# Block-sparse attention with a feed forward: gathered keys per 32 queries, unnormalised probabilities, layer norm in token layout

## The chip, the cores and the metric

The kernel runs on one core of a Trainium2 chip. The metric is the device time of one execution in microseconds. The times of before are those of three runs; the profile is of one execution.

## The reference

Four batches, eight heads, 768 positions of 64 values; blocks of 32 positions (24 a sequence). A query sees its own block and its two neighbours, the first and the last block, and three sampled blocks per query block (the same for all heads); queries of the first and the last block see everything. Then the heads are joined to 512 channels, and a layer norm and a feed forward with a residual follow.

```python
scores = scale * np.matmul(q, k.transpose(0, 1, 3, 2))
mask = np.abs(blk_i - blk_j) <= window          # window 1
mask = mask | (blk_i == 0) | (blk_j == 0) | (blk_i == n_blocks - 1) | (blk_j == n_blocks - 1)
for qb in range(n_blocks):
    for kb in sampled_blocks[qb]:
        mask[qb * block:(qb + 1) * block, kb * block:(kb + 1) * block] = True
scores = np.where(mask, scores, -1000000000.0)
...
attn = attn / (np.sum(attn, axis=-1, keepdims=True) + 1e-09)
...
xn = (x - mu) / np.sqrt(var + 1e-06) * g_ln
ch = np.maximum(xn @ w_ch1, 0.0) @ w_ch2        # 512 -> 2048 -> 512
return (x + ch).astype(np.float32)
```

## The kernel before

All matrix products are of fp16 halves: a float32 value is split in a high and a low half, and three of the four products are summed (high by high, high by low, low by high).

A **slot** is one head and 128 queries; there are 192, in order of batch, of three chunks of 256 queries (a **unit**, twelve in all), of pairs of heads. In a slot all 768 keys are scored: line 274 multiplies the stacked halves of q by the high and low halves of k, line 280 adds the low half of q by the high half of k. The result `ps` has 128 x 768. `softmax_a` adds the mask as a bias per key block (`allow`) and finds the guard of the exponent with one custom VectorE instruction (line 289), ScalarE takes the exponential with its row sum (293). `softmax_b` makes the reciprocal and a normalised high half `ph` (306), `softmax_c` the low half `pl` (314, in some slots on GpSimd, 312), and two DMA transpositions issued from SP (320, 321) put both, keys on partitions, in `pt`. `attn_v` multiplies the values by them a pair of heads at a time (332, 337), the two heads in two 64-wide column tiles, into `pa` with channels on partitions.

`layer_norm` works with channels on partitions: sums over channels are matmuls with ones (367 to 370). `ffn` is a generator that gives one matmul a step: the first layer (424) into `pu`, halves of the hidden values (434, 435), the second layer (466, 450) into `pd` with channels on partitions, the sum with the residual (409) and the store (411).

The order of issue: the main loop walks over slots. In each it issues the scores of this slot, the softmax steps of the slot before, and then a mixture of steps of the attention queue and of the feed-forward queue; `NFF` is 16 steps a slot. TensorE stands in the order as written, SP and GpSimd too in the first 27 slots; the rest is ordered by the scheduler. The loads of q, k, v, w1 and w2 are generators in an agenda by slot; k and q are cast by the GpSimd DMA queue and the low halves subtracted. Both weight matrices come as float64 bits and are split in the first 36 slots.

## Time and profile before

| | |
|---|---|
| median of 3 runs | 906.25 us (905.23 to 913.89) |
| the profiled execution | 913.7 us span, 913.89 us its own time |
| TensorE busy | 804.4 us, 6576 matmuls |
| VectorE, ScalarE, GpSimd busy | 691.0, 529.9, 288.4 us |
| DMA | 131.34 MB in 341896 packets |

Busy times are unions, so matmuls that overlap count once. Group rows give the line, the engine, the operation, the tiles, the count, the busy time, the mean of one in ns, and the idle time just before with what ended it. A matmul's mean duration contains its latency; the rate is read from start to start in the timeline. Timeline rows give the start and the length in us.

### The profile page before, as it was taken

The page shows a single profiled execution, that of the slowest core. Times are in us where ns is not written, and L with a number is a line of the kernel's source. Part 1 is how long each engine was busy: PE and PEld are TensorE (multiplying, and loading weights), DVE is VectorE, ACT ScalarE, POOL GpSimd, SP SyncE. Part 2 cuts the span into 40 slices and gives each one's busy share as a digit, 9 for nine tenths or more (in the row PEclk, how much of TensorE's full clock was granted, in tenths as well). Part 3 has the DMA queues.
Part 4 walks back from the last instruction along what each step waited for, and adds up shares of the span by engine and source line. Part 5 has one row for each costly group of instructions (what it writes and reads, how often), then busy time and mean ns, then how long its engine had stood idle before and what let it go on. Part 6 is the DMA issues. An engine that isn't in the chain of part 4 may idle for free.

```text
span 913.7 us, 17727 instructions
## 1 busy us (share of the span) xinstructions
PE 804.4 (88%) x6576; PEld 554.9 (61%) x6576; DVE 691.0 (76%) x1400; ACT 529.9 (58%) x914; POOL 288.4 (32%) x301
## 2 busy tenths in 40 slices
PE   3345568887888999999899999999999999999998
PEld 0011235554655677766567767776677777777887
DVE  6979899996467888788588788788888887883320
ACT  3566766766456765656585666656766665662120
POOL 5483656585532111154431101336321100000000
PEclk9976669997999999999989999999999999999999
DMA  8899797999997887899977776999898776662000
GB/s 214 205 261 216 148 235 188 203 177 131 165 165 141 142 126 131 135 172 178 162 126 143 141 126 127 153 163 167 161 130 145 122 118 119 105 113 42 19 6 25
DMA packets 341896, 131.34 MB, mean 144 GB/s; under 512 B 311600, under 2 KB 331184, under 8 KB 341808
## 3 DMA queue, kind: packets, MB, share of 16 engines
q1 hardware_dynamic: 329280, 108.06, 63.3%
q0 software_dynamic: 11712, 22.03, 14.2%
q8 instruction: 52, 0.85, 0.4%
q14 instruction: 36, 0.29, 0.1%
q10 hardware_dynamic: 816, 0.11, 0.1%
HBM read 60.92 MB, written 6.29 MB: 74 GB/s over the span
## 4 chain that ended last, share of the span: by engine, by line
PE 50%; DVE 7%; DMA 7%; ACT 3%; issue 3%; SPq 0%; ACTq 0%; DVEq 0%
PE pd L466 20%; PE pu L424 18%; PE pa L332 4%; DMA pt<-pl 4%; PE ps L274 3%; DMA pt<-ph 3%; PE ps L280 2%; DVE pl L314 2%; PE pa L337 2%; DVE p L289 2%; ACT p L293 2%; ACT ph L306 1%; DVE hl L435 1%; DVE xc L394 1%; DVE mua L353 0%
## 5 line engine op out<-in xcount | busy, mean ns | idle before, releaser
L314 DVE SCALAR_TENSOR_TENSOR pl<-p,st,ph 128x768 f16<-128x768 f32 x177 | 211.9, 1204 | 77.8 <-ACT ph L306 41.0
L293 ACT ACTIVATE p<-p,st 128x768 f32<-128x768 f32 x192 | 178.6, 930 | 113.9 <-DVE st L289 108.9
L306 ACT ACTIVATE ph<-p,st 128x768 f16<-128x768 f32 x177 | 162.4, 927 | 60.2 <-DMA pt<-ph 44.5
L466 PE MATMUL pd<-hl,w2h 128*128 128x256 f16 x704 | 192.4, 273 | 1.4 <-DVE hl L435 1.4
L466 PE MATMUL pd<-hh,w2h 128*128 128x256 f16 x704 | 192.7, 274 | 0.0
L466 PE MATMUL pd<-hh,w2l 128*128 128x256 f16 x704 | 192.4, 273 | 0.0
L289 DVE CUSTOM_DVE_ANT_1 p<-ps,allow 128x768 f32<-128x768 f32 x192 | 177.4, 951 | 10.4 <-PE ps L280 9.4
L424 PEld LDWEIGHTS <-w1h 128*128 128x128 f16 x1536 | 146.3, 99 | 59.5 <-issue 41.8
L274 PE MATMUL ps<-kx,qx 128*128 128x512 f16 (+1 forms) x384 | 92.3, 350 | 75.1 <-DVE st L289 57.8
L466 PEld LDWEIGHTS <-w2h 128*128 128x128 f16 x1408 | 133.6, 98 | 37.2 <-issue 22.7
L424 PE MATMUL pu<-xh,w1h 128*128 128x256 f16 x768 | 118.9, 278 | 12.8 <-DVE hl L435 8.8
L424 PE MATMUL pu<-xl,w1h 128*128 128x256 f16 x768 | 123.8, 278 | 3.0 <-DVE xl L398 3.0
L424 PE MATMUL pu<-xh,w1l 128*128 128x256 f16 x768 | 123.4, 279 | 0.0
L263 POOL TENSOR_TENSOR ql<-qr,qx 64x256 f16<-64x256 f32 x94 | 76.1, 809 | 112.3 <-issue 39.5
L332 PE MATMUL pa<-pt,vh 128*64 128x512 f16 x576 | 110.4, 408 | 0.7 <-DMA pt<-pl 0.7
L216 POOL DMA_DIRECT2D qx<-qT x48 | 26.8, 560 | 242.7 <-PE ps L274 137.1
L434 ACT ACTIVATE hh<-pu 128x512 f16<-128x512 f32 x96 | 56.2, 585 | 77.1 <-PE pu L424 77.1
L274 PEld LDWEIGHTS <-qx 128*128 128x128 f16 x384 | 37.1, 100 | 102.2 <-issue 76.9
L435 DVE SCALAR_TENSOR_TENSOR hl<-pu,hh 128x512 f16<-128x512 f32 x96 | 65.7, 685 | 30.9 <-ACT hh L434 30.6
L424 PEld LDWEIGHTS <-w1l 128*128 128x128 f16 x768 | 75.2, 100 | 18.9 <-issue 9.2
L337 PE MATMUL pa<-pt,vl 128*64 128x256 f16 x576 | 84.2, 287 | 0.0
L466 PEld LDWEIGHTS <-w2l 128*128 128x128 f16 x704 | 68.9, 98 | 15.4 <-issue 7.7
(95 smaller groups left out, 933.6 us busy)
## 6 DMA issues: line engine op xcount, KB each, us to landing
qr<-qs SPq DMA_DIRECT2D x48, 128.0 KB, 3.1
kx<-kT POOLq DMA_DIRECT2D x16, 384.0 KB, 6.3
qx<-qT POOLq DMA_DIRECT2D x48, 128.0 KB, 3.5
raw<-w SPq DMA_DIRECT2D x12, 512.0 KB, 4.3
out<-ot SPq DMA_DIRECT2D x48, 128.0 KB, 2.4
vr<-v POOLq DMA_DIRECT2D x24, 192.0 KB, 3.7
raw<-ks POOLq DMA_DIRECT2D x12, 384.0 KB, 4.4
w2l<-w SPq DMA_DIRECT2D x4, 1024.0 KB, 6.2
```

What stands on the lines that cost most here:

```text
L263: eng.tensor_sub(ql[rows], qr[rows], qx[rows, j])
L274: nc.tensor.matmul(s.ps[:, lo:hi], qx[:, s.h % 2, s.qs], kx[:, s.h % 2, lo:hi], start=True, stop=False)
L289: nc.vector.tensor_tensor_reduce(out=s.p.rearrange(blk, k=BLK), in0=s.ps[:, 0:S].rearrange(blk, k=BLK), in1=bias, scale=-0.125, scalar=3.0 ...
L293: nc.scalar.activation(s.p, s.p, AF.Exp, bias=s.st[:, 0:1], scale=-1.0, accum_out=s.st[:, 2:3])
L306: nc.scalar.activation(ph, s.p, AF.Copy, scale=st[:, 3:4])
L314: nc.vector.scalar_tensor_tensor(out=pl, in0=s.p, scalar=st[:, 3:4], in1=ph, op0=ALU.mult, op1=ALU.subtract)
L332: nc.tensor.matmul(pa[hh * D : (hh + 1) * D, 0 : 2 * CH], vh[:, hh, t, :], pts[hh][:, t].rearrange("p i n -> p (i n)"), start=t == 0, stop ...
L337: nc.tensor.matmul(pa[hh * D : (hh + 1) * D, 0:CH], vl[:, hh, t, :], pts[hh][:, t, 0, :], start=False, stop=t == KT - 1, skip_group_check= ...
L424: nc.tensor.matmul(ph[:, j * CH : (j + 1) * CH], w[:, ct, fs], x[:, ct, :], start=n == 0, stop=n == 3 * CT - 1, skip_group_check=True)
L434: nc.scalar.activation(dh, ph[:, 0 : 2 * CH], AF.Relu)
L435: nc.vector.scalar_tensor_tensor(out=dl, in0=ph[:, 0 : 2 * CH], scalar=0.0, in1=dh, op0=ALU.max, op1=ALU.subtract)
L466: nc.tensor.matmul(po, w[:, f, es], x[:, f, :], start=n == 0, stop=n == 3 * FT - 1)
```

## The change

The kernel is rewritten around **units of 32 queries**. 88 units (blocks 1 to 22 of four batches) make 22 sparse tiles of four units; the queries of the first and last blocks make two dense tiles. A **slot** is one tile and head: 24 x 8 = 192 and a pause of 8.

- Scores: a unit's keys are its 256 own ones. Three neighbouring blocks are read where the keys lie (`kx`), the first, the last and the three sampled blocks are copied beside each other (`kg`) by `gather_k`, one tile ahead: 16 copies from SP, 12 of them from an address that SP first reads as a register (`value_load`). Each unit is a matmul of 32 columns wide output (tile of 32 partitions in PSUM).
- Values are split, written to DRAM with both halves in a row (`vrow`), and the 256 rows of a unit are fetched by two indirect DMAs of GpSimd (`gather_v`, 8 a tile).
- Softmax: the exponent carries the factor 4096, the halves `ph` and `pl` are those of the unnormalised exponential, made for a pair of heads at once, and the reciprocal is applied after the product with the values, which now has tokens on partitions.
- Layer norm by VectorE's statistics instructions with tokens on partitions; its halves are transposed by DMA for the first layer. g is folded into w1. The second layer has the hidden values as the stationary operand and 512 output channels as columns: 1152 matmuls of 512 columns instead of 2304 of 256.
- SP, GpSimd and TensorE stand in the written order throughout the main loop. All keys of a batch are loaded before its first slot. Feed forward begins in slot 27, 24 steps a slot, 384 steps for a group of two tiles (16 slots); a second-layer matmul counts two steps.

```diff
+    LAG = 6
+    FF0 = 27
+    NFF = 24
...
+    def gather_k(t):
...
+        t.kg = kgp.tile([P, 4, 5, H * BLK], F16, tag="kg", name=f"kg{t.i}")
+        for u, (b, i) in enumerate(t.units):
+            kx = kx_s[b % 2]
+            nc.sync.dma_start(t.kg[:, u, 0:2, :], kx[:, 0 : NB : NB - 1, :])
+            for r in range(NR):
+                n = (i - 1) * NR + r
+                reg = nc.sync.value_load(ss_i[0:1, n : n + 1, 0], min_val=0, max_val=NB - 1)
+                nc.sync.dma_start(t.kg[:, u, 2 + r : 3 + r, :], kx[:, bass.ds(reg, 1), :])
...
+    def gather_v(t):
+        t.vg = vgp.tile([P, 4, 2, H, P], F16, tag="vg", name=f"vg{t.i}")
+        for u, (b, i) in enumerate(t.units):
+            for j, idx in enumerate((ia, ib)):
+                nc.gpsimd.indirect_dma_start(
+                    t.vg[:, u, j].rearrange("p h d -> p (h d)"), None, vrow[b],
+                    bass.IndirectOffsetOnAxis(ap=idx[:, i - 1 : i].bitcast(U32), axis=0),
+                )
...
+        for n, q in enumerate((t.qx, t.ql)):
+            for k in range(2):
+                for u, (b, i) in enumerate(t.units):
+                    rows = slice(u * BLK, (u + 1) * BLK)
+                    if k == 0:
+                        dst, rhs = pr.ps[rows, h % 2, 0:3], kx_s[b % 2][:, i - 1 : i + 2, hs]
+                    else:
+                        dst, rhs = pr.ps[rows, h % 2, 3:8], t.kg[:, u, :, hs]
+                    nc.tensor.matmul(dst, q[:, h, rows], rhs,
+                                     start=n == 0 and k == 0 and h % 2 == 0,
+                                     stop=n == 1, skip_group_check=True)
...
+        for k in range(n):
+            nc.scalar.activation(pr.e[:, k], pr.e[:, k], AF.Exp, bias=st[:, 1, h0 + k : h0 + k + 1],
+                                 scale=-1.0, accum_out=st[:, 2, h0 + k : h0 + k + 1])
...
+        nc.scalar.copy(pr.ph, e)
+        nc.vector.tensor_sub(pr.pl, e, pr.ph)
...
+    def transposes(pr):
+        n, W = len(pr.heads), S if pr.t.kind == "d" else 256
+        pr.pT = ptp.tile([P, 2, n * W // P, P], F16, tag="pt", name=f"pt{pr.i}")
+        nc.sync.dma_start_transpose(out=pr.pT[:, 0], in_=pr.ph)
+        nc.sync.dma_start_transpose(out=pr.pT[:, 1], in_=pr.pl)
...
+        for k in range(nk):
+            for i in range(2):
+                for rows, vv in parts:
+                    w = D if i else P
+                    nc.tensor.matmul(t.xa[rows, h % 4, 0:w], pr.pT[:, i, k0 + k, rows],
+                                     vv[:, k, 0:w], start=first and k == 0 and i == 0,
+                                     stop=k == nk - 1 and i == 1, skip_group_check=True)
...
+        nc.vector.bn_stats(ls[:, 0:6], x)
+        nc.vector.bn_aggr(ls[:, 8:10], ls[:, 0:6])
...
+    def ln_transposes(gr):
+        gr.xT = lnp.tile([P, 2, CT, 2 * P], F16, tag="xT", name=f"xT{gr.i}")
+        for j, t in enumerate(gr.tiles):
+            ts = slice(j * P, (j + 1) * P)
+            nc.sync.dma_start_transpose(out=gr.xT[:, 0, :, ts], in_=t.xh)
+            nc.sync.dma_start_transpose(out=gr.xT[:, 1, :, ts], in_=t.xl)
...
+                for n, (w, x) in enumerate(((w2h, hh), (w2l, hh), (w2h, hl))):
+                    nc.tensor.matmul(po, x[:, f, ts], w[:, f, :], start=f == 0 and n == 0,
+                                     stop=f == FT - 1 and n == 2)
+                    if f < FT - 1 or n < 2:
...
+    for t in tiles:
+        if t.i:
+            at(once(gather_k, t), t.first - (4 if t.n == 5 else 7))
+        if t.i > 1:
+            at(once(load_q, t), t.first - 6)
...
+            at(once(gather_v, t), t.first - 2)
...
+            run(i)
+            if i < NS and slots[i]:
+                scores(slots[i])
+                pr = slots[i].pr
+                if slots[i] is pr.slots[-1]:
+                    softmax(pr)
+            if 0 < i <= NS and slots[i - 1] and slots[i - 1] is slots[i - 1].pr.slots[-1]:
+                transposes(slots[i - 1].pr)
+            if 0 <= i - LAG < NS and slots[i - LAG]:
+                s = slots[i - LAG]
+                attn_v(s)
+                if s.h == H - 1:
+                    gr = groups[s.t.i // 2]
+                    layer_norm(s.t, gr, s.t.i % 2)
+                    if s.t.i % 2:
+                        lnq.append((i + 1, gr))
```

What stands on SP in the middle of the program before: the transpositions of the probabilities (`pt`), now and then a store (`out`) or a load of q (`qr`).

```order
L320 DMA_TRANSPOSE pt_4_4435<-ph_4431 128x6x128
L411 DMA out<-ot_0_4402 128x256
L321 DMA_TRANSPOSE pt_4_4435<-pl_4433 128x6x128
L320 DMA_TRANSPOSE pt_5_4498<-ph_4494 128x6x128
L321 DMA_TRANSPOSE pt_5_4498<-pl_4496 128x6x128
L411 DMA out<-ot_1_4531 128x256
L256 DMA qr_5631<-qs 128x256
```

And on SP in the middle of the changed program, at the end of a group of two tiles: a store, the probabilities of the third pair of heads, the four transpositions of the layer norm (`xT`), those of the fourth pair, and the beginning of the next tile's run of key copies (`kg`).

```order
L471 DMA out<-x_4987 128x512
L374 DMA_TRANSPOSE pt_6957<-ph_6883 128x4x128
L375 DMA_TRANSPOSE pt_6957<-pl_6884 128x4x128
L427 DMA_TRANSPOSE xT_6978<-xh_6321 128x4x128
L428 DMA_TRANSPOSE xT_6978<-xl_6322 128x4x128
L427 DMA_TRANSPOSE xT_6978<-xh_6913 128x4x128
L428 DMA_TRANSPOSE xT_6978<-xl_6914 128x4x128
L374 DMA_TRANSPOSE pt_7100<-ph_7034 128x4x128
L375 DMA_TRANSPOSE pt_7100<-pl_7035 128x4x128
L274 DMA kg_7146<-kx_130 128x2x256
L277 TENSOR_LOAD ss_i
L277 ISA x2
```

The run then goes on with twelve such register loads (`ss_i` holds the numbers of the sampled blocks) and sixteen copies up to the next load of q; before, nothing but single loads and stores stood between two transpositions.

TensorE of the changed program at the same place, where the probabilities by values of a tile's first head (`pa`) end and the first layer of a new group (`pu`) begins:

```order
L395 MATMUL pa_0_6961<-vg_6352,pt_6723 32x64
L395 LDWEIGHTS pt_6723
L395 MATMUL pa_0_6961<-vg_6352,pt_6723 32x64
L444 LDWEIGHTS w1h
L444 MATMUL pu_0_6985<-xT_6978,w1h 128x256
```

Both read a transposition of the list above: `pt_6723` stands directly behind the run of key copies, `xT_6978` behind the store and three pairs of heads. Before, the first layer of a unit followed its layer norm at a distance of some slots.

789 lines of the change are left out of this document (362 added, 427 removed).

## The prediction

> **What bounds the kernel now.** I read the page's first two parts, then the timeline of TensorE and of the SP queue, then the waits. Engine shares, slices, and the ending chain:
>
> ```profile
> PE 804.4 (88%) x6576; PEld 554.9 (61%) x6576; DVE 691.0 (76%) x1400; ACT 529.9 (58%) x914; POOL 288.4 (32%) x301
> PE   3345568887888999999899999999999999999998
> PEclk9976669997999999999989999999999999999999
> PE 50%; DVE 7%; DMA 7%; ACT 3%; issue 3%; SPq 0%; ACTq 0%; DVEq 0%
> ...
> 0.00:122.00 122.00, 54.28 (x204) 16.67 (x205) 103.53 (x176) 74.64 (x120) 68.24 (x58) 0.79 0.93 215
> 122.00:914.00 792.00, 750.15 (x6372) 538.19 (x6371) 587.52 (x1226) 455.25 (x795) 220.18 (x243) 0.97 0.76 133
> ```
>
> There are two stages. To 122 us TensorE is busy 54 us of 122 and VectorE 104: attention alone, held by the softmax and by loads. Afterwards TensorE is busy 750 us of 792 (42 us idle, clock 0.97): matmuls set the time. The boundary and the price of a feed forward come from these:
>
> ```profile
> 10.07 0.82 PE L274 MATMUL ps<-kx,qx 128*128 128x512 f16 x2 [10.07 <-DMA qx<-qT]
> 122.56 1.01 PE L424 MATMUL pu<-xh,w1h 128*128 128x256 f16 x4 [3.90 <-ACT xh L397]
> 868.17 20.96 PE pu L424 x192
> 889.13 20.97 PE pd L466 x192
> ```
>
> One unit of 256 queries costs 41.9 us, 0.109 per 256-column matmul, so twelve cost 503 of the 791 us from 122.56 on. In those 791 us stand also:
>
> ```profile
> L332 PE MATMUL pa<-pt,vh 128*64 128x512 f16 x528 | 96.3, 391 | 0.7 <-DMA pt<-pl 0.7
> L274 PE MATMUL ps<-kx,qx 128*128 128x512 f16 x332 | 72.4, 329 | 16.3 <-DVE st L289 16.0
> L280 PE MATMUL ps<-kx,ql 64*128 64x512 f16 (+1 forms) x332 | 52.3, 333 | 0.0
> 500.54 0.27 PE L466 MATMUL pd<-hl,w2h 128*128 128x256 f16 x1
> 500.74 0.30 PE L337 MATMUL pa<-pt,vl 128*64 128x256 f16 x2
> 500.87 0.38 PE L332 MATMUL pa<-pt,vh 128*64 128x512 f16 x2
> 501.09 0.28 PE L337 MATMUL pa<-pt,vl 128*64 128x256 f16 x2
> 501.20 0.38 PE L332 MATMUL pa<-pt,vh 128*64 128x512 f16 x2
> 501.41 0.28 PE L337 MATMUL pa<-pt,vl 128*64 128x256 f16 x2
> 501.62 0.28 PE L466 MATMUL pd<-hh,w2l 128*128 128x256 f16 x1
> ```
>
> Start to start, the pair of 512-column matmuls at 500.87 takes 0.22 us, the time of one: the two 64-wide column tiles run side by side. The pair at 501.09 takes 0.11. A change of tiling costs 0.1 us more each way (500.54 to 500.74 and 501.41 to 501.62 instead of 0.11). So probabilities by values cost 44 x 6 x 0.32 = 85 us, and 166 heads of scores 166 x 0.33 for L274 and 40 for L280 (half of a pair's time where two heads run side by side) = 95. What is left of 791 is 103: some 38 of tiling changes, and 65 of waits and half-clock stretches.
>
> **The change on TensorE.** The feed forwards keep their columns: the first as it was, the second 1152 matmuls of 512 columns at 0.22 instead of 2304 of 256. Nothing is gained. A head of 128 queries now has four units side by side in 32-wide column tiles: scores 2 x (96+160) columns = 0.215 us, probabilities by values 2 x (128+64) = 0.16, if four tiles run together as two do here. After the feed forward has begun, 165 heads of scores and 171 of values give 36 + 27, and 12 more for the sixteen dense heads (1536 columns two at a time instead of 512 four at a time, and 1152 instead of 384): 75 instead of 180, **-105 us**. The four-way overlap is not in this trace. Its ends are no gain from four over two (+63) and this value; I take this, because the two-way row is a whole doubling. Tiling changes stay at two a head, 38 us.
>
> **VectorE, ScalarE, GpSimd.**
>
> ```profile
> L216 POOL DMA_DIRECT2D qx<-qT x48 | 26.8, 560 | 242.7 <-PE ps L274 137.1
> L434 ACT ACTIVATE hh<-pu 128x512 f16<-128x512 f32 x96 | 56.2, 585 | 77.1 <-PE pu L424 77.1
> L435 DVE SCALAR_TENSOR_TENSOR hl<-pu,hh 128x512 f16<-128x512 f32 x96 | 65.7, 685 | 30.9 <-ACT hh L434 30.6
> L380 DVE TENSOR_TENSOR xc<-xT,mup 128x256 f32<-128x256 f32 x48 | 16.9, 414 | 1.8 <-PE mup L370 1.3 <-PE mup L367 0.4
> L343 ACT ACTIVATE xT<-pa 128x256 f32<-128x256 f32 x48 | 17.7, 369 | 3.7 <-PE pa L337 3.7
> L293 ACT ACTIVATION_READ_ACCUMULATOR p<-p,st 128x1 f32 x192 | 36.0, 187 | 0.0
> L231 POOL TENSOR_TENSOR kx<-raw,kx 64x768 f16<-64x768 f32 x30 | 55.8, 1862 | 20.5 <-DMA kx<-kT 12.1 <-DMA pt<-pl 5.6 <-DMA raw<-ks 1.4
> ```
>
> A pair of heads is now two reductions of 256 (0.41 each), two exponentials (0.37 + 0.19), a cast of 512 (0.6), a difference of 512 (0.69): 1.5 us of VectorE and 1.7 of ScalarE. A tile of eight heads, with its other steps, needs some 15 us of each, while TensorE needs 8 x (2.62 + 0.215 + 0.16 + 0.2) = 25.6. That relief is worth nothing after 122 us, since these engines already hide behind TensorE. As latency the chain stays: 0.8 + 1.1 + 0.6 + 0.7, small steps, hand-overs and queueing, some 5.5 us from the second head's scores to both halves. GpSimd's eight gathers, a price the trace lacks, lie between its plain DMA issue (0.56, L216) and a 64x1024 subtraction (2.5, scaled from L231): 4 to 20 us a tile, under 25.6, taken as hidden; at the upper end the values would come just late.
>
> **The SP queue: the new path.**
>
> ```profile
> L320 SPq EVENT_SEMAPHORE  x191: 17/17/3954, 10.9 to 825.3; - x191
> L321 SPq DMA_TRANSPOSE pt<-pl x192: 1209/1237/3938, 19.6 to 827.0; - x192
> DMA to landing us min/median/max: 2.7/3.0/10.1
> 524.13 0.53 SPq L256 DMA_DIRECT2D qr<-qs  x1
> out<-ot SPq DMA_DIRECT2D x48, 128.0 KB, 2.4
> raw<-w SPq DMA_DIRECT2D x12, 512.0 KB, 4.3
> ```
>
> A copy holds SP 0.5 us, a 128x768 transpose 1.22, so a 128x512 one 0.85 (0.81 by size, 1.22 if it is fixed). Per sparse tile SP issues 16 key copies of the next tile in one run, 12 of them behind a register load and three register instructions, and no transposition can pass it. The copies are 8 us. No row shows the register load; the nearest are the semaphore instruction (0.02) and the shortest round trip of a DMA (2.4). I take 0.75 with its three register instructions, near the 0.53 of the row that is nearest in kind: a burst of 8 + 9 = **17 us** (bounds 8 to 37). "DMA: Bandwidth & Descriptors" of the Trainium skill, section "Latency and other measured facts", gives a register load a floor of about 600 ns, which no trace here shows; by it alone the burst were 15 and the sum below some 36 us lower.
>
> The loop of a tile: the burst B, the query load 0.5, then the first pair's two transpositions, landing 0.85 + 2.7 later; the waiting values, this slot's feed forward and the next scores 3.2; the softmax 5.5 until SP may begin the next burst. That is B + 13 against 25.6, so SP decides from B = 12.7, and eighteen such tiles in the long stage cost 18 x 4.3 = **+77 us**. Behind the burst wait all transpositions; for them wait TensorE's values, and in order behind those the feed forward.
>
> Layer norm: the queue gives each group exactly 16 slots of 24 steps, the production rate, so from the third group on a feed forward starts in the slot right after its layer norm. After the old group's last matmul SP still has: the output (0.7 on VectorE and 0.35), a pair's transpositions 1.7, four for the group 3.4, landing 1.9. Of these 8 us, 1.5 are covered (scores, values, the last transposition needed later): 6.5 us of wait. After a wait TensorE runs slowly for a while:
>
> ```profile
> 143.93 0.48 PE L274 MATMUL ps<-kx,qx 128*128 128x512 f16 x2 [2.47 <-DVE st L289]
> 145.60 1.06 PE L424 MATMUL pu<-xl,w1h 128*128 128x256 f16 x4
> 146.46 1.06 PE L424 MATMUL pu<-xh,w1h 128*128 128x256 f16 x4
> ```
>
> Four matmuls take 0.86 instead of 0.44 for some 4 us, so +2.2. Ten groups x 8.7 = **+87**, and the last, with nothing else to run, +10. The layer norm's own removal (5 us of ones matmuls) is within the rounding.
>
> **The start.** All keys of batch 0 come first, six 512 KB blocks through two buffers. SP's twelve register loads stand ahead of the second block (to 12 us); each further two blocks take 4.3 + 1.05 (cast, twice the columns of L434) + 2.5 = 8; then four value tiles go through one buffer, 4.4 each (cast, difference, 2.8 for the write); the last key copy of tile 0 lands at some 52 us, where scores began at 10. Then tile 1's burst; the first transposition near 69. Two and a half tiles follow at 17 + 4 x 1.7 + 4 = 28 until slot 27: the feed forward begins near 142 instead of 122.6, **+20** (between -10 with free register loads and +60 at the upper price).
>
> **The sum**, against this execution's 913.7 us (its own time is 913.9, 7 above the median of the three): 913.7 + 20 - 105 - 65 (the old waits) + 77 + 87 + 10 = 938. Less those 7: **931**, 2.7% over the median.
>
> **Rivals.** Measurement tells about 1% from no change.
> (1) The burst is short, B under 12.7 (a register load with its instructions under 0.4 us): the 77 go, and three bursts ahead of the feed forward are 4 shorter each: 931 - 77 - 13 = **841**, faster. Between, up to B = 14.5 the change still gains over 1%. For it: the semaphore instruction costs 0.02, and VectorE's relief leaves no other limit.
> (2) Dear register work, 1.0 us: B = 20, 18 x 3 + 9 more: **994**.
> (3) The small matmuls are paced by their weight loads. Upper price by rows: a load and matmul in the 501.09 pair, 0.055; sixteen take 0.88. 336 heads x 0.69 = 232 more, but a slot of 4.6 hides the burst (-77): **1086**. "TensorEngine Tiling (Array Packing)" of the Trainium skill, "Restrictions and Gotchas", says that column tiling disables fast weight loading, which speaks against this change; 500.74 and 501.09 show no load exposed at 64 columns.
> (4) DMA engines fill up:
>
> ```profile
> GB/s 214 205 261 216 148 235 188 203 177 131 165 165 141 142 126 131 135 172 178 162 126 143 141 126 127 153 163 167 161 130 145 122 118 119 105 113 42 19 6 25
> DMA packets 341896, 131.34 MB, mean 144 GB/s; under 512 B 311600, under 2 KB 331184, under 8 KB 341808
> q1 hardware_dynamic: 329280, 108.06, 63.3%
> ```
>
> The transposed bytes halve (384 of 197 KB, 75 MB, to 36), but key copies (88 units x 5 blocks of 64 KB, 29), gathered values (176 of 256 KB, 46) and other loads and stores (67 instead of 56) bring some 178 MB. At this kernel's mean that would be 1236 us, at the 261 GB/s of its best slice 682: if landings grow by 3 us, twenty tiles add 60: **991**. Against it: packets of 512 bytes and more replace the 256-byte ones of the transpositions.
>
> **How the numbers follow.** Forecast (B of 15 to 18.5: 895 to 958) 0.44; rival 1 with all shorter bursts 0.36; rival 2 0.11; rivals 3 and 4 0.09. Faster by over 1% is rival 1 and a sliver of the forecast (0.38), within 1% is B of 14.5 to 15.6 (0.13), slower the rest (0.49). Signs are split, so the range spans both: 838 (rival 1) to 1005; the forecast's own is 895 to 958.
>
> **What would show it.** SP's time between a tile's first and last key copy (17), and TensorE idle before L395 that ends with a transposition; TensorE idle before L444 of some 6 us at ten places; first scores near 52, first L444 near 142; four 96-column matmuls within 0.05 us. I am wrong if the burst passes in 12 us, if LAG covers it anyway, or if GpSimd's gathers end the waits before L395.

## The result and the profile after

The changed kernel takes **1257.7 us** (median of four runs, 1249.3 to 1266.5); four runs of the kernel before on the same chip gave 908.0 us (905.2 to 913.9). The ratio is 1.383, 95% interval 1.373 to 1.393: the change makes the kernel 38% slower. Forecast was 931, with a range from 838 to 1005: the sign was right, the size missed by 326 us. In e6_poolq, e7_combo, e10_best and e11_best2 below, one or two of the four executions were in a slower state, and their medians are of the others (the recorded expectations use the medians of all four, 1038.6 and 962.7 for e7_combo and e11_best2).

The page of the changed kernel, first its engine shares, TensorE's slices, clock and DMA, then the chain that ended last:

```profile
PE 723.9 (57%) x9600; PEld 452.0 (36%) x9600; DVE 473.9 (37%) x1152; ACT 373.7 (30%) x849; POOL 313.5 (25%) x251
PE   0101236834848741782784734475876682884988
PEclk9999757877879875986896867688887896996989
DMA packets 257572, 179.59 MB, mean 142 GB/s; under 512 B 162097, under 2 KB 224690, under 8 KB 257458
SPq 35%; DMA 22%; PE 17%; DVE 9%; issue 8%; ACT 5%; POOL 2%; ACTq 1%; DVEq 0%; POOLq 0%
```

Before, TensorE led that chain with 50% and SP's queue had 0%; now SP's queue leads and TensorE has 17. The two stages, cut at the first feed forward, by busy time of each engine, then granted clock, DMA share and GB/s:

```profile
53.00:180.60 127.60, 22.92 (x794) 18.01 (x795) 72.49 (x151) 50.23 (x121) 61.80 (x44) 0.84 0.85 213
180.60:1264.70 1084.10, 699.60 (x8800) 433.33 (x8800) 383.08 (x968) 307.26 (x706) 241.12 (x198) 0.81 0.55 132
```

The long stage was 792 us with 42 idle at clock 0.97; now it is 1084 with 384 idle at clock 0.81. And it begins at 180.6 instead of 122.6. What TensorE waited for (total, times, longest):

```profile
PE pa L395 <- DMA pt<-ph: 230.7, 28, 23.1
PE pu L444 <- DMA xT<-xh: 152.9, 11, 31.5
PE ps L323 <- DMA kg<-kx: 48.7, 8, 19.5
```

So it waits for transpositions: of probabilities ahead of the values (L395), of the normalised rows ahead of the feed forward (L444). Why they come late is seen on SP's queue. Here is one quiet tile, from the fourth pair's transpositions through the burst of key copies to the layer norm (start, length):

```profile
849.85 1.39 SPq L374 DMA_TRANSPOSE pt<-ph  x1
851.34 1.23 SPq L375 DMA_TRANSPOSE pt<-pl  x1
852.62 0.68 SPq L274 DMA_DIRECT2D kg<-kx  x1
854.56 2.92 SPq L278 DMA_DIRECT2D kg<-kx  x3
...
867.89 3.13 SPq L278 DMA_DIRECT2D kg<-kx  x3
...
872.24 1.24 SPq L374 DMA_TRANSPOSE pt<-ph  x1
...
878.15 1.22 SPq L374 DMA_TRANSPOSE pt<-ph  x1
879.46 1.21 SPq L375 DMA_TRANSPOSE pt<-pl  x1
880.72 1.26 SPq L427 DMA_TRANSPOSE xT<-xh  x1
...
884.71 1.31 SPq L428 DMA_TRANSPOSE xT<-xl  x1
```

And TensorE in the same window; the number in brackets is the idle time before a row and what ended it:

```profile
868.97 0.23 PE L323 MATMUL ps<-kx,qx 128*32 128x96 f16 x4
...
876.26 0.30 PE L395 MATMUL pa<-vg,pt 128*32 128x128 f16 x4 [6.88 <-DMA pt<-ph]
...
890.33 1.04 PE L444 MATMUL pu<-xT,w1h 128*128 128x256 f16 x4 [13.14 <-DMA xT<-xh]
```

The burst runs from 852.62 to 871.02. The probabilities that were ready in that time are transposed from 872.24 on, behind an output and a query load, and TensorE, in its written order, stands 6.9 us for them. At the end of the tile the old feed forward is through, SP still has an output, two transpositions of a pair and four of the group, and TensorE stands 13.1 us.

A third place is not in the prediction: the refills of keys and values for batches 1 to 3. Here SP in the refill of the values of batch 2:

```profile
715.88 0.53 SPq L247 DMA_DIRECT2D vr<-v  x1
721.67 4.50 SPq L256 DMA_DIRECT2D vrow<-vs  x2
726.26 1.80 SPq L374 DMA_TRANSPOSE pt<-ph  x1
...
739.02 4.01 SPq L256 DMA_DIRECT2D vrow<-vs  x2
...
752.04 1.24 SPq L374 DMA_TRANSPOSE pt<-ph  x1
```

Each store stands right behind its load in the written order, so SP waits for landing, cast and difference, and the transpositions at 726 and 752 wait behind such stores. In the waits of SP's own queue these stores have a row of their own:

```profile
SPq L256 <- DVE vs L252: 81.2, 18, 8.9
```

### The profile page after: what moved, and what is told of

Its sections match the earlier page's. It is cut to its first block, busy times and chain, and to the rows that moved or that the text cites. A ratio compares the mean times of both kernels' runs of the same rounds, so it can differ in the third digit from the quotient of the medians.

```text
span 1264.7 us, 24225 instructions
## 1 busy us (share of the span) xinstructions
PE 723.9 (57%) x9600; PEld 452.0 (36%) x9600; DVE 473.9 (37%) x1152; ACT 373.7 (30%) x849; POOL 313.5 (25%) x251
## 4 chain that ended last, share of the span: by engine, by line
SPq 35%; DMA 22%; PE 17%; DVE 9%; issue 8%; ACT 5%; POOL 2%; ACTq 1%; DVEq 0%; POOLq 0%
SPq L278 10%; PE pu L444 8%; SPq L277 8%; PE po L463 7%; SPq L375 5%; SPq L274 4%; SPq L374 4%; DMA vr<-v 3%; DMA qr<-qT 3%; DMA xT<-xh 2%; DMA pt<-ph 2%; DMA kr<-kT 2%; DMA xT<-xl 2%; DMA vrow<-vs 2%; DVE pl L364 2%
## 5 line engine op out<-in xcount | busy, mean ns | idle before, releaser
L444 PE MATMUL pu<-xT,w1h 128*128 128x256 f16 x1536 | 241.3, 297 | 157.3 <-DMA xT<-xh 152.9
L395 PE MATMUL pa<-vg,pt 128*32 128x64 f16 (+1 forms) x2816 | 74.6, 225 | 271.5 <-DMA pt<-ph 230.7
L444 PEld LDWEIGHTS <-w1h 128*128 128x128 f16 x1536 | 155.1, 106 | 194.5 <-DMA xT<-xh 149.2
L364 DVE TENSOR_TENSOR pl<-e,ph 128x512 f16<-128x512 f32 (+1 forms) x104 | 104.2, 1002 | 205.9 <-ACT ph L363 154.4
L395 PEld LDWEIGHTS <-pt 128*32 128x32 f16 (+1 forms) x3200 | 59.7, 105 | 302.7 <-DMA pt<-ph 264.7
L463 PE MATMUL po<-w2h,hh 128*128 128x512 f16 x384 | 155.9, 406 | 1.7 <-ACT w2h L212 1.7
L463 PE MATMUL po<-w2l,hh 128*128 128x512 f16 x384 | 154.5, 402 | 2.0 <-POOL w2l L214 2.0
L463 PE MATMUL po<-w2h,hl 128*128 128x512 f16 x384 | 153.6, 400 | 0.0
L358 ACT ACTIVATE e<-e,st 128x256 f32<-128x256 f32 (+1 forms) x192 | 102.8, 536 | 150.9 <-DVE st L355 130.3
L444 PE MATMUL pu<-xT,w1l 128*128 128x256 f16 x768 | 129.6, 297 | 0.0
L285 POOL DMA_INDIRECT vg<-vrow,ia x88 | 90.5, 1028 | 61.2 <-issue 38.8
L285 POOL DMA_INDIRECT vg<-vrow,ib x88 | 87.2, 991 | 26.8 <-issue 26.8
L444 PEld LDWEIGHTS <-w1l 128*128 128x128 f16 x768 | 82.0, 107 | 15.3
L323 PE MATMUL ps<-kg,qx 128*32 128x160 f16 x704 | 48.2, 252 | 48.7 <-DMA kg<-kx 48.7
```

What stands on the lines that cost most here:

```text
L285: nc.gpsimd.indirect_dma_start(t.vg[:, u, j].rearrange("p h d -> p (h d)"), None, vrow[b], bass.IndirectOffsetOnAxis(ap=idx[:, i - 1 : i]. ...
L323: nc.tensor.matmul(dst, q[:, h, rows], rhs, start=n == 0 and k == 0 and h % 2 == 0, stop=n == 1, skip_group_check=True)
L358: nc.scalar.activation(pr.e[:, k], pr.e[:, k], AF.Exp, bias=st[:, 1, h0 + k : h0 + k + 1], scale=-1.0, accum_out=st[:, 2, h0 + k : h0 + k ...
L364: nc.vector.tensor_sub(pr.pl, e, pr.ph)
L395: nc.tensor.matmul(t.xa[rows, h % 4, 0:w], pr.pT[:, i, k0 + k, rows], vv[:, k, 0:w], start=first and k == 0 and i == 0, stop=k == nk - 1 a ...
L444: nc.tensor.matmul(ph[:, j * N : (j + 1) * N], w[:, ct, fs], gr.xT[:, i, ct, :], start=n == 0, stop=n == 3 * CT - 1, skip_group_check=True)
```

## The experiments

All start from the changed kernel (1257.7 us). Differences below are from it; with intervals of about 0.01 of the ratio a difference is good to some 12 us, so that those of e9_merge, e12_now1 and e17_halfgather are hardly clear of it. The runs were made in five groups, each with runs of the kernel before beside it (medians 908 to 913 us); reckoned by the ratios, the differences change by up to 9 us.

| run | what is edited | us | ratio to before, 95% | difference |
|---|---|---|---|---|
| e1_spread | key copies in four pieces | 1186.1 | 1.298 (1.288 to 1.307) | -72 |
| e2_static | no register loads | 1176.4 | 1.283 (1.273 to 1.294) | -81 |
| e3_slack | feed forward four slots later | 1190.3 | 1.304 (1.293 to 1.316) | -67 |
| e4_norefill | no refills | 1152.0 | 1.263 (1.253 to 1.274) | -106 |
| e5_latev | values' stores in later slots | 1223.2 | 1.338 (1.329 to 1.348) | -34 |
| e6_poolq | key copies on GpSimd's queue | 1176.9 | 1.285 (1.272 to 1.297) | -81 |
| e8_none | e1 to e4 together | 942.3 | 1.036 (1.027 to 1.046) | -315 |
| e9_merge | one transposition for both halves | 1240.6 | 1.366 (1.356 to 1.377) | -17 |
| e12_now1 | 6 MB of weight loads left out | 1243.7 | 1.370 (1.359 to 1.381) | -14 |
| e13_nocopy | no key copies | 1060.7 | 1.164 (1.159 to 1.169) | -197 |
| e14_nolow | no transpositions of low halves | 1154.7 | 1.266 (1.259 to 1.273) | -103 |
| e17_halfgather | half of the gathers of values | 1235.9 | 1.356 (1.348 to 1.364) | -22 |
| e18_statichalf | e2 and e17 | 1118.5 | 1.230 (1.222 to 1.238) | -139 |
| e7_combo, e10_best, e11_best2, e15_best3, e16_best4 | versions with the same output | 1035.8, 971.3, 951.4, 978.4, 968.3 | 1.142, 1.077, 1.048, 1.073, 1.058 | -222, -286, -306, -279, -289 |

### The burst: in pieces, without registers, on another queue, gone

**e1_spread**, where the burst of a tile becomes four pieces:

```diff
...
-            at(once(gather_k, t), t.first - (4 if t.n == 5 else 7))
+            for u, k in enumerate((8, 6, 4, 2)):
+                at(once(gather_k, t, (u,)), t.first - (4 - u if t.n == 5 else k))
```

> Same work; the 16 key copies of the next tile are issued in four pieces of 4 copies, 8, 6, 4 and 2 slots ahead of the tile, not in one run. Changed kernel 1257.7 us. Theory A (order: the 17.7 us burst stands ahead of the transpositions): no transposition waits for more than about 4.5 us, the wait of 6 to 7 us ahead of the values goes at some twenty tiles and some of the layer norm's too: 1257 - 20 x 6 = about 1135. Rival B (amount: SP must issue 17.7 us of copies, 9.8 of transpositions, 2.5 for layer norm and 1 of other issues for each tile, 31 us, however it is ordered): a quiet tile falls only from 34.6 to 31 or 32: about 1190 to 1210. Rival C (the time is in the refills of keys and values and in layer norm's waits): no change, 1240 to 1265.

Measured 1186.1, just under rival B's 1190 to 1210 and far from theory A's 1135. Waits of TensorE:

```profile
PE pu L447 <- DMA xT<-xh: 197.2, 11, 39.2
PE ps L326 <- DMA kg<-kx: 131.0, 23, 20.0
PE pa L398 <- DMA pt<-ph: 58.5, 17, 16.9
```

The wait ahead of the values falls from 230.7 to 58.5, as order would have it; but the copies now come late for the scores (48.7 to 131.0) and layer norm's wait rises from 152.9 to 197.2. Almost three quarters of what the order gave (127 of 172 us) is taken back at two other places.

**e2_static**, fixed addresses:

```diff
-                n = (i - 1) * NR + r
-                reg = nc.sync.value_load(ss_i[0:1, n : n + 1, 0], min_val=0, max_val=NB - 1)
-                nc.sync.dma_start(t.kg[:, u, 2 + r : 3 + r, :], kx[:, bass.ds(reg, 1), :])
+                nc.sync.dma_start(t.kg[:, u, 2 + r : 3 + r, :], kx[:, 5 * r + 4 : 5 * r + 5, :])
```

> The three sampled blocks of each unit are copied from fixed places (blocks 4, 9, 14), so that no register is loaded; the copies keep number and size, and the output is that of other blocks. Left out per tile on SP: 12 x (register load 0.27 + its register instructions 0.22), about 5.9 us. Theories A (order) and B (amount) both expect about 20 x 6 = 120 us less, some 1135; if register loads cost more than their own instructions (SP drained around each), the burst falls from 17.7 to under 10 and the time below 1100. Rival C (refills and layer norm's waits set the time): under 30 us less, over 1225.

Measured 1176.4, 81 us less than the changed kernel, not 120: layer norm's wait rises here too, to 176.6 us, and the group's transpositions land later. Landing times of `xT` (issue to landing, least, median, most), of the changed kernel, then of this one:

```profile
DMA to landing us min/median/max: 2.4/4.3/8.8
```

```profile
DMA to landing us min/median/max: 2.4/7.7/10.5
```

**e6_poolq** moves the copies and their register loads to GpSimd's queue:

```diff
-            nc.sync.dma_start(t.kg[:, u, 0:2, :], kx[:, 0 : NB : NB - 1, :])
+            nc.gpsimd.dma_start(t.kg[:, u, 0:2, :], kx[:, 0 : NB : NB - 1, :])
...
-                reg = nc.sync.value_load(ss_i[0:1, n : n + 1, 0], min_val=0, max_val=NB - 1)
-                nc.sync.dma_start(t.kg[:, u, 2 + r : 3 + r, :], kx[:, bass.ds(reg, 1), :])
+                reg = nc.gpsimd.value_load(ss_i[0:1, n : n + 1, 0], min_val=0, max_val=NB - 1)
+                nc.gpsimd.dma_start(t.kg[:, u, 2 + r : 3 + r, :], kx[:, bass.ds(reg, 1), :])
```

> Same work; the key copies with their register loads are issued on GpSimd's queue instead of SP's. SP then has for each tile 8 transpositions, 4 of the layer norm per pair of tiles and two plain copies: 13 us. Theory (SP's issue time of the copies, 17.7 us a tile, is what delays the transpositions): if GpSimd issues a copy as fast as its 0.56 us for a plain DMA, its load per tile is 8 gathers 8 us, 16 copies 9, registers 6, the query's difference 2: 25 us beside 25.6 of TensorE, and the time falls by 80 to 130 us, to 1130 to 1180. Rival (GpSimd in order is as bad a place: the copies wait behind the query's difference, which waits for ScalarE, and the gathers behind the copies): a gain under 30 us or a loss.

Measured 1176.9. After the first feed forward (at 210.0) 970 us are left instead of 1084, a gain of 114; but that first feed forward comes 29 us later than in the changed kernel. GpSimd's instructions stand in the written order too, and TensorE now waits 86.1 us for the copies instead of 48.7; what holds the start isn't taken apart.

**e13_nocopy** reads five blocks in place and copies nothing.

```diff
-        if t.kind == "d":
-            return
+        return
         t.kg = kgp.tile([P, 4, 5, H * BLK], F16, tag="kg", name=f"kg{t.i}")
...
-                        dst, rhs = pr.ps[rows, h % 2, 3:8], t.kg[:, u, :, hs]
+                        dst, rhs = pr.ps[rows, h % 2, 3:8], kx_s[b % 2][:, 3:24:5, hs]
```

> No key copies at all: the five copied blocks of every unit are replaced by blocks 3, 8, 13, 18, 23, read in place (the output is that of other blocks). So the burst B is 0 instead of 17.7 us a tile; all else stays. Theory (a quiet tile is B + 17 us of transposition, values, scores and softmax in turn, or TensorE's 25.6, whichever is longer): 34.6 falls to 26 to 28, some twenty tiles, and less in the waits of layer norm and of the refills: 150 to 200 us less, 1060 to 1110. Rival (the time without copies is set by layer norm and refills, as pieces gave only 71 us less): 1160 to 1190.

Measured 1060.7, as the theory has it. A pair of quiet tiles, first of the changed kernel (83 us), then of this one (67):

```profile
807.00:890.00 83.00, 56.65 (x800) 35.51 (x800) 30.04 (x82) 23.39 (x60) 21.03 (x20) 0.83 0.57 139
```

```profile
659.00:726.00 67.00, 53.80 (x799) 34.78 (x797) 27.66 (x82) 23.09 (x60) 21.76 (x20) 0.88 0.71 145
```

What waits are left in it:

```profile
PE pu L443 <- DMA xT<-xh: 156.0, 11, 27.3
PE pa L394 <- DMA pt<-ph: 84.6, 17, 15.8
```

In the pair from 659 on nothing is left but layer norm's wait. The burst's whole share, with its bytes and its part in the start (the first feed forward begins at 163.2), is 197 us.

### Layer norm's wait and the refills

**e3_slack**:

```diff
...
-                ffq.append(ffn(gr))
+                late.append((i + 4, gr))
+            if late and late[0][0] <= i:
+                ffq.append(ffn(late.pop(0)[1]))
```

> Same work; each feed forward starts four slots after its layer norm instead of in the next slot, so that TensorE has four slots of scores and values while the transpositions of the normalised rows are issued and land. Theory of layer norm's wait (153 us ahead of L444, 11 waits): the wait goes at the places where steps of the old feed forward are left to spread, and those slots are only attention: gain 60 to 130 us, 1130 to 1200. Rival: the attention slots themselves wait for SP (transpositions behind the burst), so the same SP work is waited for at L395 instead of L444: within 20 us of 1257.

Measured 1190.3. The wait ahead of L444 is gone (152.9 to 15.2 and 11.9 for the two halves), but the one ahead of L395 rises:

```profile
PE pa L395 <- DMA pt<-ph: 287.0, 34, 25.7
```

So the gain is 67 and not 125. Part of the wait changed its place. A reading that fits, which no run tests by itself: the slots that now run without a feed forward ask for their transpositions sooner, and SP isn't quicker.

**e4_norefill**:

```diff
...
-        at(load_k(b), KAT[b])
-        at(load_v(b), VAT[b])
+        pass
```

with batch 0's keys and values read in all places.

> Left out: keys and values of batches 1 to 3 are neither loaded nor split; every unit uses those of batch 0. So SP issues no load or store of a refill and waits for none. Theory of the refills (SP waits in its order for a staging buffer, a cast or a store of the refill, and the transpositions wait behind it): the three long tiles (69.8 start apart: 83.2, 78.2, 88.9 us) fall to the 35 to 50 of their neighbours: 3 x 40 = 120 us less, about 1135. Rival (SP's issue time of the burst sets these tiles too, refills only fill its gaps): under 40 us less, over 1215.

Measured 1152.0. The refills cost 106 us, and the prediction had no term for them. The tile pairs with a refill shrink (125.6 us from one feed forward's start to the next becomes 85), the quiet ones stay at 83 to 86.

**e5_latev** keeps the refills and only moves the values' stores into later slots:

```diff
-    VAT = {1: 36, 2: 77, 3: 116}
+    VAT = {1: 28, 2: 69, 3: 108}
...
+                if b:
+                    yield
                 nc.sync.dma_start(vrow[b][rows, :], vs.rearrange("p h d -> p (h d)"))
```

> Same work; in the refills of the values of batches 1 to 3, SP issues the load of 256 rows in one slot and the two stores of the split values in the next two slots, not right behind the load; the refill begins eight slots earlier so that it ends when it did. In the changed kernel SP stands some 9 us at each of these loads (load to second store, 715.9 to 726 and so on), 9 loads, 80 us. Theory (SP's order: the stores wait for load, cast and difference, and the next tile's transpositions stand behind them): 50 to 80 us less than 1257. Rival (what costs is the refills' transfers and casts themselves, wherever they are issued): within 20 us of 1257.

Measured 1223.2: 34 us less, outside both expectations. The wait of SP for the split values (81.2 us) falls only to 57.4: with a single `vs` buffer the second half is split only after the first half's store has landed, and ScalarE's wait for that landing stays (41.1 us before the edit, 41.4 after). So the place of the stores is a third of the refills' price; the rest isn't taken apart by these runs.

**e8_none** has e1, e2, e3 and e4 at once.

> All suspected causes out at once: no refills (batch 0's keys and values for all units), sampled blocks from fixed places (no register loads), copies in four pieces, feed forward four slots later; the output is not the reference's. If the causes add up and account for the miss: 1257 - 106 - 67 - some 110 (order and register loads together) = about 970, within 40 us of the prediction of 931. If it stays over 1030, a further cause is missing (TensorE's clock, the fixed 1.22 us of each transposition, the slower start).

Measured 942.3. The page, and the stage from the first feed forward on:

```profile
PE 685.4 (73%) x9600; PEld 441.5 (47%) x9600; DVE 445.9 (47%) x1134; ACT 343.4 (36%) x813; POOL 272.7 (29%) x233
170.00:941.00 771.00, 661.47 (x8800) 422.49 (x8800) 349.97 (x947) 273.40 (x662) 197.35 (x176) 0.93 0.73 160
```

The four single gains are 72 + 81 + 67 + 106 = 326 (by the ratios 347); together they give 315. They add up to within a tenth, so they are four prices and not one wait counted four times. This stage is now 21 us shorter than the 792 of before; what is left against it is the start, 170 instead of 122.

That 942 lies 11 us from the forecast of 931 is chance and doesn't make the account complete. This run also lacks the burst's and layer norm's waits, 77 + 13 + 87 us of that forecast, so by the forecast's own sums it would take some 754. The start is 41 us later than these sums would have it (170 against 129), TensorE is busy 661 us against some 620, and it is idle for 110 against 10, 72 of them ahead of the matmuls on `kg`: the copies in pieces come late.

### Is it SP's amount of work, or what stands behind it?

**e9_merge** turns both halves with one transposition, half as many in all:

```diff
-        nc.sync.dma_start_transpose(out=pr.pT[:, 0], in_=pr.ph)
-        nc.sync.dma_start_transpose(out=pr.pT[:, 1], in_=pr.pl)
+        nc.sync.dma_start_transpose(out=pr.pT.rearrange("p a b q -> p (a b) q"),
+                                    in_=pr.pp.rearrange("p a k -> p (a k)"))
```

> Same output; the high and the low half of a pair's probabilities stand in one tile and are turned by one transposition of 128x1024 instead of two of 128x512, and so are the two halves of the normalised rows: 128 transpositions instead of 256. Theory (SP's issue time sets the pace, and a transposition's 1.22 us is fixed, as 128x512 and 128x768 both take it): SP issues 128 x 1.24 = 159 us less, 6.2 a tile, as much as without register loads (81 us less there), and layer norm's wait is shorter too: 80 to 120 us less, 1140 to 1180. Rival (the issue goes by bytes, 2.4 us for the merged one, and the high half now waits for the low one): 1250 to 1275.

Measured 1240.6. The transposition of 128x1024 has nearly the same issue time (1.30 us median against 1.22), so the theory's premise holds and its forecast fails: 128 issues less gave 17 us, not 80 to 120. The tile's rows, of the issue (least, median, most in ns) and of the landing, then the first row of SP's waits:

```profile
L374 SPq DMA_TRANSPOSE pt<-ph x104: 1231/1298/10192, 76.7 to 1170.6; - x104
...
DMA to landing us min/median/max: 3.0/4.3/8.4
```

```profile
SPq L374 <- DVE ph L364: 262.3, 46, 17.3
```

About half of the freed time, some 150 us, is seen again as waiting: all waits of SP ahead of the probabilities' transpositions add up to 243 us in the changed kernel and to 322 here, 262 of them for the low half. And the landing rose from 2.7 to 4.3 us. In **e14_nolow** the low half isn't turned at all, and the high half goes when it is ready.

```diff
...
-        nc.sync.dma_start_transpose(out=pr.pT[:, 1], in_=pr.pl)
...
-            nc.sync.dma_start_transpose(out=gr.xT[:, 1, :, ts], in_=t.xl)
```

> Left out: the transpositions of the low halves of the probabilities and of the normalised rows; the matmuls use the high half twice, so the output is not the reference's. As with the merged transpositions, 128 of them and 159 us of SP's issue are gone, but here the high half doesn't wait for the low one and half the bytes are turned. Merged gave 17 us less. If that was because issue time in itself doesn't count: 1230 to 1245 again. If merging gave its gain back by waiting for the low half (0.7 us) and by landing later (4.3 us instead of 2.7): 60 to 110 us less, 1150 to 1200.

Measured 1154.7, a gain of 103: the same number of issues less, but no wait for the low half and half the bytes. `xT` lands in 2.5 us, layer norm's wait is 102.2 instead of 152.9, and the first feed forward begins 14 us earlier; the wait ahead of the values doesn't fall (241.2 against 230.7). So SP's total by itself isn't the price; the length of the chain counts: the last input ready, issue, landing. Whether the gain over e9_merge comes from the bytes or from not waiting for the low half isn't separated.

**e17_halfgather** and **e18_statichalf** leave out half of the gathers on GpSimd's queue:

```diff
-            for j, idx in enumerate((ia, ib)):
+            for j, idx in enumerate((ia,)):
```

> Left out: the second of the two gathers of values of each unit (88 of 176, 23 MB); the matmuls use the first one's rows twice, so the output is not the reference's. Theory (the gathers of a tile run just when layer norm's transpositions are under way, and their bytes lengthen those landings and the probabilities'): median landing of xT 4.3 us falls to about 3, layer norm's wait of 153 us to 120 or 130, the waits ahead of the values by some 30: 30 to 60 us less than 1257. Rival (gathers hidden, as the prediction had it): within 15 us.

> Both: sampled blocks from fixed places (no register loads: 1176.4 alone) and only the first gather of values. Without register loads SP was 118 us quicker, but the time fell by 81 only, while layer norm's wait rose from 153 to 177 us and the landing of xT from 4.3 to 7.7. If the gathers' bytes took that gain back: xT lands in about 4, the wait falls under 150, and the time to 1110 to 1135. If not: 1160 to 1180.

e17_halfgather measured 1235.9, 22 us less and between the two expectations, but not by the theory's way: `xT` still lands in 4.8 us, and the wait ahead of the values rises to 262.1. e18_statichalf measured 1118.5, which is 58 less than e2_static alone, as the theory has it. There `xT` lands in 2.5 us instead of 7.7, and layer norm's wait is 147.5 instead of 176.6. So the gathers were all but hidden while SP was slow; once it is quicker, they take back part of the gain. The landing times speak for their 256 KB each, which run beside the group's transpositions; GpSimd's issues, left out with them, aren't separated from the bytes.

**e12_now1** leaves out six of the eight loads of the first weight:

```diff
...
-            raw = (w2g[:, 0:4096], w2g[:, 4096:8192], w2f[:, 4096:8192])[(i - 2) % 3]
+            raw = kept[i % 2]
...
+        if i < 2:
             nc.sync.dma_start(raw.rearrange("p (c f) t -> p c (f t)", c=CT),
```

> Left out: six of the eight loads of the first weight (1 MB each; the blocks already loaded are used again, so the output is not the reference's). It tells what holds the start, where the first feed forward began at 180.6 us and not at 142. Theory (DMA engines are full, 0.86 to 0.95 of them from 53 to 180 us): 6 MB at some 210 GB/s, first feed forward 25 us earlier, and 1257 - 25. Rival (SP's bursts and the chain from the values' store to their gather hold it): first feed forward within 8 us of 180, time within 12 us.

e12_now1 measured 1243.7; the first feed forward begins at 170.5 instead of 180.6: 10 us, where full DMA engines would have given 25. Without register loads it begins at 165.9, without key copies at 163.2, in e8_none at 170.1. Bytes and SP each hold the start by 10 to 17 us; no single run takes more than 20 of the 58 us away.

### Versions with the same output

**e7_combo** has the copies in pieces (8, 7, 6 and 4 slots ahead), the later feed forward, the later stores, and reads the first and last block in place:

```diff
-            nc.sync.dma_start(t.kg[:, u, 0:2, :], kx[:, 0 : NB : NB - 1, :])
...
+                    elif k == 1:
+                        dst, rhs = pr.ps[rows, h % 2, 3:5], kx_s[b % 2][:, 0 : NB : NB - 1, hs]
```

> Same output; four edits together: key copies in four pieces (8, 7, 6, 4 slots ahead), feed forward four slots later, values' stores in later slots, and the first and last block, which every unit uses, are read in place by a matmul of their own instead of being copied (88 copies of 128 KB at 0.65 us fewer, 57 us of SP; 64 + 96 columns instead of 160). If the effects add: 1257 - 71 - 67 - 65 - 30 = about 1025. If they are one and the same wait counted three times: 1100 to 1150. Below 908 only if nothing but TensorE's own time is left, which a start of some 160 us and 640 us of matmuls at full clock would give (about 830).

**e10_best** adds the merged transpositions and buffers (`stg` 3, `vsp` 2); **e11_best2** puts the sampled copies of two units on GpSimd's queue:

```diff
+                eng = nc.gpsimd if u >= 2 else nc.sync
```

**e15_best3** and **e16_best4** vary the distance of values and feed forward and load the small tables from GpSimd's queue.

> Same output; the four edits of the combination (1038.6) with the merged transpositions, a third staging buffer and a second one for split values. SP's issue per tile falls from some 27 us to 20, under TensorE's 25.6, so the waits ahead of the values (87 us) and ahead of the scores (39) should mostly go: 930 to 980. If the merged transposition takes twice as long: 1030 to 1050.

> As the run before, and the sampled copies of two of the four units of a tile are issued on GpSimd's queue: SP has 14 us a tile, GpSimd some 21. If SP's amount still counts at 20 us a tile: 20 to 40 us less than the run before, and perhaps below 908; if it no longer does, or the copies on GpSimd wait behind the query's difference and come late for the scores: the same or up to 30 us more.

> Same output; the fastest version so far (962.7: pieces, blocks read in place, merged transpositions, half of the sampled copies on GpSimd, values' stores later, third staging buffer), with the values of a head eight slots behind its scores instead of six, the feed forward five slots later, and the small tables loaded from GpSimd's queue so that ScalarE's first cast isn't held to 15 us. The waits ahead of the values (46 us) and of the feed forward (42) should go by half, the start by 5 to 10: 905 to 930. If DMA engines (0.81 to 0.99 busy there) set the landings: 950 to 970.

> As the run before, but values six slots behind their scores as in the changed kernel, the feed forward six slots later. Waits ahead of the feed forward go, those ahead of the values stay: 920 to 945. If DMA engines set the landings: 950 to 970.

Measured 1035.8, 971.3, **951.4**, 978.4 and 968.3. The first three keep their expectations or miss them by some 11 us; the last two miss the 905 to 930 and 920 to 945 that were expected of them and do not gain over e11_best2. The fastest is 306 us faster than the changed kernel and still 4.8% slower than before (ratio 1.034 to 1.062). No version beat the kernel before. What TensorE waits for most in e10_best is still the transpositions of probabilities:

```profile
PE pa L401 <- DMA pt<-ph: 125.1, 33, 13.7
```

So e10_best's number came in without its reason: the waits ahead of the values, which the expectation had mostly go, were 85.8 + 39.2 us for the two halves in e7_combo and are as long here. Whether that is the DMA engines or the order isn't settled.

## Why the prediction was right and wrong

**Right.** TensorE's work: a head's scores and values and the feed forward behind them at full clock, in e4_norefill:

```profile
611.26 0.23 PE L323 MATMUL ps<-kx,qx 128*32 128x96 f16 x4
...
611.49 0.34 PE L395 MATMUL pa<-vg,pt 128*32 128x128 f16 x16
611.77 0.61 PE L444 MATMUL pu<-xT,w1h 128*128 128x256 f16 x4
```

From the first row to the feed forward are 0.51 us, against 0.215 + 0.16 + 0.2 forecast; four column tiles run together, and rival 3, weight loads that set the pace, is out. "TensorEngine Tiling (Array Packing)" of the Trainium skill, "Restrictions and Gotchas", says that fast weight loads are lost with column tiles; by these rows nothing of that shows. The burst: 17.3 to 19.1 us a tile after the first feed forward against 17, so rivals 1 and 2 are out. That decided the sign; the 0.75 for a register load with its instructions was a choice within wide bounds (8 to 37 us for the burst), and that it came so near is partly luck. Its parts, by the source rows of the two lines:

```profile
L277 SPq TENSOR_LOAD <-ss_i x264: 263/272/794, 2.8 to 1135.5; - x132
L277 SPq FUSED_REGOPS  x264: 147/152/187, 3.4 to 1135.8; - x132
L278 SPq DMA_DIRECT2D kg<-kx x264: 485/494/1208, 41.8 to 1136.2; - x132
```

The load itself is 0.27; with its register instructions and the gaps a step of the burst costs about 0.73 ((2.92 - 3 x 0.49) / 2), the 0.75 of the forecast. The floor of about 600 ns that "DMA: Bandwidth & Descriptors" of the Trainium skill, "Latency and other measured facts", gives is not kept by the load alone. First scores near 52: the matmuls on `kg` begin at 45.4 with the high half of q and at 56.0 with the low one (those on `kx` already at 19.5). Bytes: 179.6 MB against 178. (What is left of the 791 us is 108 by the prediction's own terms, not 103; this changes nothing.)

**Wrong**, in four steps, the first the largest, and in two smaller terms named behind them:

1. **Refills: no term.** "The change on TensorE" and "The SP queue" count the tile's own issues; the loads and stores of batches 1 to 3 stood in no sum. They cost 106 us (e4_norefill). The changed kernel's order on SP has them, each store of values right behind its load; only their bytes were counted, under rival 4.
2. **"The loop of a tile ... B + 13".** The burst ahead of the one shown above begins and ends so:

```profile
818.70 0.69 SPq L274 DMA_DIRECT2D kg<-kx  x1
...
836.56 0.53 SPq L263 DMA_DIRECT2D qr<-qT  x1
```

From its end to the fourth pair's transpositions are 13.3 us (836.56 to 849.85), as forecast. But behind them SP issues this pair's own two, 2.8 us (849.85 to 852.62), before it can begin the next burst: the loop is B + 16, 33.9 us from one burst's start to the next (818.70 to 852.62) and not 30. TensorE's wait ahead of the values is 6.2 us in the first of these two tiles and 6.9 in the second, where 4.3 were forecast. The forecast gave the burst 77 + 13 in all; taken away whole it gives 197 (e13_nocopy), which holds what refills and start lose by it too.
3. **Layer norm: "of these 8 us, 1.5 are covered".** Measured 13.1: two transpositions of the pair 2.6, four of the group 5.3 (880.72 to 886.02), landing 4.3, output and VectorE's sum the rest, nothing covered. A transposition of 128x512 costs what one of 128x768 did, 1.22 and here 1.26; the forecast took 0.85 by size and named 1.22 as the other end. And 1.9 for the landing was under the shortest of the `pt` rows (2.7). Ten groups by 6.6 us would be 66.
4. **The start: 142.** Measured 180.6, 39 later. Forecast were 69 for the first transposition and 28 us for each of the two and a half tiles behind it. The first transposition starts at 76.3, and from there on 104 us pass. In the first of these tiles the transpositions themselves take two to four times as long on SP as elsewhere, with loads of weights among them; the DMA engines are 85% busy from 53 us to the feed forward. Six loads less gave 10 us (e12_now1); the rest of this term stays open:

```profile
81.66 2.60 SPq L374 DMA_TRANSPOSE pt<-ph  x1
84.35 5.17 SPq L375 DMA_TRANSPOSE pt<-pl  x1
...
90.25 3.91 SPq L374 DMA_TRANSPOSE pt<-ph  x1
```

How far these terms go is seen in the trace of e4_norefill, where the refills are out. The forecast's own sums leave 795 us for the long stage: some 620 of TensorE's work at full clock (616 by 503 + 75 + 38), 22 of slow clock behind ten waits, and 152 of waiting (77 ahead of the values, 65 and 10 for layer norm). Measured, the stage from the first feed forward on and its longest waits:

```profile
180.00:1145.00 965.00, 679.59 (x8800) 426.23 (x8800) 361.66 (x950) 277.99 (x670) 204.29 (x180) 0.85 0.56 129
```

```profile
PE pu L444 <- DMA xT<-xh: 133.2, 11, 15.7
PE pa L395 <- DMA pt<-ph: 108.1, 17, 12.5
PE ps L307 <- DVE st L341: 20.4, 5, 8.1
```

With the waits for the low halves (2.3 and 11.5) layer norm's is 60 us over the forecast and the values' 43. TensorE is busy some 40 us longer. Ahead of the scores of the two dense tiles (L307) it waits 20 us for VectorE, for which the forecast, with the dense heads priced on TensorE alone, had no term. With the start, 39, these are 202 us; with the refills, 106, 308 of the 326. The rest is small waits and the noise between runs.

TensorE's longer time fits its clock. In the changed kernel it was busy 700 us in the long stage. "TensorE: Matmul & The Clock Gate" of the Trainium skill, Part 1, says that TensorE falls to half its clock after some 3.4 us of idleness and needs as long to come back. The trace agrees: behind the wait of 13.14 us shown above, the 256-column matmuls run at half pace for 3.3 us (890.33 to 893.63). A pair of quiet tiles with waits of 6.2, 6.9 and 13.1 us is granted 0.83, one with a single wait of 13.3 us 0.88, and the long stage of e8_none, idle for 14% of its time in many shorter waits, 0.93. So a wait costs more than its own length, and the forecast priced that behind layer norm's waits alone.

Rival 4, full DMA engines, did not decide (share 0.55 in the long stage); whether the improved versions run into it isn't settled (0.73 in e8_none). That "GpSimd's gathers" are hidden held for the changed kernel up to 22 us.

## What to carry to other kernels

When a change moves work to an in-order queue, price the whole queue over the whole program, with the occasional refills that stand in the same order, and not one iteration of its loop. An instruction count on such a queue is not a price: some 150 us of issue saved gave 17 where the input was still awaited, and 103 where it wasn't and half the bytes were gone too; ask for the chain from the last input to the landing. And where four removals each give about 80 us, run them all at once: whether they add up tells whether they are separate causes. Whether the account is complete is another question, and it is answered only by the forecast's sum without the terms that were taken out.

## What the runs showed of the hardware

- A DMA transposition holds SP for 1.22 us at 128x512 and at 128x768, and 1.30 at 128x1024: the issue is all but fixed, while the landing grows (2.7 to 4.3 us for twice the bytes). In the first tile of the start, with loads of weights among them, one of 128x512 held it for up to 5.17 us.
- The 16 matmuls of a head's scores in four 32-wide column tiles take 0.23 us (611.26 to 611.49 in e4_norefill): four run side by side, as two 64-wide ones did before.
- A register load on SP takes 0.27 us, about 0.73 in all with what goes with it; a copy from a register's address costs 0.49, no more than the same copy from a fixed address (0.60 in e2_static).
- An indirect DMA of 128 rows of 2 KB costs GpSimd some 0.95 us of issue and lands after 6.3 us.
